# Pacing the pieces of one batch's convolution anew inside an MLP loop

## The chip, the cores and the metric

The kernel runs on one core of a Trainium2 chip. The metric is device time in microseconds (us) of one execution, the median of several. TensorE is called PE here, VectorE DVE, ScalarE ACT, GpSimd POOL and SyncE SP, as in the profile.

## The reference

Two sequences (`B = 2`) of `S = 12480` tokens with 128 channels go through a long convolution with a filter that a small network makes, are gated, and go through an MLP with 2048 hidden units:

```python
h_filt = (np.maximum(pos_emb @ w1, 0) @ w2) * np.exp(-0.01 * pos)[:, None]
u = x * v
y = irfft(rfft(u, 2 * S, axis=1) * rfft(h_filt, 2 * S, axis=0), 2 * S, axis=1)[:, :S]
z = (x * y).reshape(B * S, 128)
h = z @ moe_w_in                       # 128 -> 2048
out = np.maximum(0.01 * h, h) @ moe_w_out
```

## The kernel before

**The convolution** is done as matrix products with constant tables, in two stages and a return. Stage 1 of a batch makes 98-point transforms of 64 columns of tokens, stage 2 joins them across 128 partitions, multiplies them by the filter's spectrum and goes back; the last step of the return, one product per tile (`front`, L679), is part of the MLP's preparation. Batch 0's convolution and the filter's spectrum come first, before any MLP work, together with the preparation of the weights.

**The MLP** runs over `total = 64` tiles of 390 tokens, 32 for each batch (`NT = 32`), and in each tile over `NF = 16` blocks of 128 hidden units. One block is `m1(t, f)` (L689: three matmuls into a tile of tag `mh`, of which there are three; then ACT makes `rh`, the rounded relu, L698, and DVE the remainder `rl`, L699) and `m2` of the block three places earlier (L712 to L714: three matmuls into `acc`). Within a tile other work is inserted by block number `f`, counted from 0: at `f` = 2, 5 and 7 the output of the tile before (`finish`: copy L719; four transposes L723 and the copy L725; the DMAs out L730), at 6 the additions `join(t + 1)` on POOL (L484, L485), at 9 the transposes and copy for `xs` (L671, L673), at 12 the product `yp` (L679), `zf`, `zh` and `zl` (L684 to L686). At the start of a tile `load_tile(t + 1)` puts the loads `g`, `xm` and `cin` (L464 to L473) on SP's queue.

**Batch 1's convolution** is a Python generator, `conv = conv1()`. Each `next(conv)` emits one piece, what stands between two `yield`s. Its first stage works on 16 chunks (`N1`), each in two halves of four pieces; the 16 matmuls of a half (L350) are in its second piece. At a chunk's first piece `fetch_a(c + 1)` puts the next chunk's loads on SP's queue (`ft` L165, `xv` L67 and L69), and `late()` puts the store of the chunk before there (L363). At the fifth piece `mult_a(c + 1)` multiplies the loaded x and v on POOL (L178). The second stage, `conv1b`, works on 25 chunks (`NCH`) of 15 pieces each, between a start of eight pieces and short first and last chunks. In order, with letters that are used below, a chunk's pieces are: O (loads L376 and L379, store L148), A (six matmuls into a pair of PSUM tiles, L416; those of A and F have line L132 in the profile, that of the helper `three`), then per half s of the pair

```python
nc.scalar.mul(us[L, s, :w], up[s][H, :w], -1.0)                      # B (s=0), D (s=1)  L426
nc.vector.tensor_tensor(out=p1[:, s, :w], in0=up[s][:, :w], ...)     # B, D              L427
yield
nc.scalar.copy(us[H, s, :w], up[s][L, :w])                           # C, E              L429
yield
nc.gpsimd.tensor_tensor(out=us[:, s, :w], ...)                       # D, F     L431, L432
```

then F (`back`, six matmuls of the chunk before, into the next pair of PSUM tiles), G and H (two copies, L154), I, J and K (`ph` on ACT L444, `pl` on POOL L445), L, M and N (`split` of the next chunk: `th` on ACT L389 and L393, `tl` on DVE L394; `tl` of the first half in M, of the second in N). A and F use one pair of tiles (tag `cv`, two buffers), so each waits until the other's results have been read.

**The order of work** is written out by hand (`tc.manual_schedule()`): every engine runs its instructions in the order in which the Python code emits them. Eight halves of stage 1, `AHEAD = 32` pieces, are emitted before the MLP's first block. During batch 0's tiles a counter `slots` goes up by one per block, and after each block (behind its `m1`, `m2` and inserted work) as many pieces are emitted as the pace asks for. `pieces` is 498, an estimate of the generator's length; the rest is emitted by the same rule, and by `run(conv)` in tile 31. `SLOTS` is 512.

Of the kernel before, what the change touches and what calls it, by code (L numbers as in the profile page):

```python
# [21 lines left out]
MC1 = 4  # L22
# [5 lines left out]
def tile_conv_mlp(ctx, tc, x, v, pos_emb, w1, w2, w_in, w_out, cf, cr, cg, cb, ci, cw, out):  # L28
# [34 lines left out]
    def load_tokens(t, src, m0, n):  # L63

        full = src[: ROWS * NB, :].rearrange("(a p n) d -> a p n d", p=2, n=HB)
        for r in (slice(0, R0), slice(R0, ROWS)):
            nc.sync.dma_start(out=t[r], in_=full[r, :, m0:m0 + n, :])  # L67
        last = src[ROWS * NB + m0:ROWS * NB + m0 + n, :]
        nc.sync.dma_start(out=t[ROWS:], in_=last[None, None, :, :].to_broadcast([1, 2, n, last.shape[1]]))  # L69
# [34 lines left out]
    def run(g):  # L104
        for _ in g:
            pass
# [51 lines left out]
    with tc.manual_schedule():  # L158
# [3 lines left out]
        def fetch_a(c):  # L162
            ft = s0.tile([128, MC1 * 4 * NA], F32, tag="s0", name="ft1", bufs=3)[:NA].rearrange(
                "a (m p e) -> a m p e", m=MC1, p=2)
            nc.sync.dma_start(out=ft, in_=cf[:, c * MC1:(c + 1) * MC1])  # L165
            xv = []
            for i, src in enumerate((x, v)):
                t = s0.tile([128, 1024], F32, tag=f"s{1 + i}", name="xv1", bufs=3 - i)[:NA, :2 * MC1 * D].rearrange(
                    "a (p m d) -> a p m d", p=2, d=D)
                load_tokens(t, src[1], c * MC1, MC1)  # L170
                xv.append(t)
            got[c] = ft, xv
# [158 lines left out]
        N1 = HB // MC1  # L331
# [121 lines left out]
        pieces = N1 * (MC1 // 2) * 4 + 20 + 14 * NCH  # L453
        A0, A1, A2, A3, A4, A5 = 2, 2, 1, 1, 1, 1
        AHEAD = 4 * (A0 + A1 + A2 + A3 + A4 + A5)
# [5 lines left out]
        def load_tile(t):  # L461
            b, mp = divmod(t, NT)
            g = mlp.tile([NA, 2, 2, 2, NA], F32, tag="g", name="g")
            nc.sync.dma_start(out=g, in_=cg[:, mp])  # L464
            xt = mlp.tile([NA, 2, 2, D], F32, tag="xm", name="xm")
            full = x[b, :ROWS * NB, :].rearrange("(a p n) d -> a p n d", p=2, n=HB)
            for r in (slice(0, R0), slice(R0, ROWS)):
                nc.sync.dma_start(out=xt[r], in_=full[r, :, 2 * mp:2 * mp + 2, :])
            r0 = ROWS * NB + 2 * mp
            nc.sync.dma_start(out=xt[ROWS:, 0], in_=x[b, None, r0:r0 + 2, :])  # L470
            ci_t = mlp.tile([NA, 2, 2, 2, D], F32, tag="cin", name="cin")
            k1 = NA if t else (NCH - 2) * KC
            nc.sync.dma_start(out=ci_t[:k1].rearrange("k r m p d -> k r (m p d)"),  # L473
                              in_=scr2[b][:k1, :, 2 * mp:2 * mp + 2, :].rearrange("k r m e -> k r (m e)"))
            ld[t] = (ci_t, g, xt)

        def join(t):

            ci_t, g, xt = ld[t]
            cp = mlp.tile([NA, 2, 2, 2, D], F32, tag="cp", name="cp", bufs=1)  # L480
            c0, c1 = (ci_t[:, :, :, i, :].rearrange("k r m d -> k (r m) d") for i in range(2))
            o0, o1 = (cp[:, :, :, i, :].rearrange("k r m d -> k (r m) d") for i in range(2))
            eng = nc.gpsimd if t else nc.vector
            eng.tensor_tensor(out=o1, in0=c0, in1=c1, op=ALU.subtract)  # L484
            eng.tensor_tensor(out=o0, in0=c0, in1=c1, op=ALU.add)  # L485
            ld[t] = (cp, g, xt)

        with ExitStack() as st:
# [111 lines left out]
            for c in range(NCH):  # L600
# [14 lines left out]
                for ri in range(2):  # L615
                    for k in range(n):
                        i, j = 64 * (k % 2), ri * n // 2 + k // 2
# [71 lines left out]
        def m1(t, f):  # L689
            zh, zl = z[t]  # L690
            hp = ps.tile([128, TOK], F32, tag="mh", name="mh", bufs=3)
            fs = slice(f * 128, f * 128 + 128)
            nc.tensor.matmul(hp, w_in_h[:, fs], zh, start=True, stop=False)  # L693
            nc.tensor.matmul(hp, w_in_h[:, fs], zl, start=False, stop=False)  # L694
            nc.tensor.matmul(hp, w_in_l[:, fs], zh, start=False, stop=True)  # L695
            rh = sm.tile([128, TOK], F32R, tag="rh", name="rh", bufs=5)
            rl = sm.tile([128, TOK], F32R, tag="rl", name="rl", bufs=5)
            nc.scalar.activation(out=rh, in_=hp, func=AF.Relu)  # L698
            nc.vector.scalar_tensor_tensor(out=rl, in0=hp, scalar=0.0, in1=rh, op0=ALU.max, op1=ALU.subtract)  # L699
            return rh, rl  # L700

        def m2(t, f, r):
            rh, rl = r
            if f == 0:
                zh, zl = z[t]
                ap = ps.tile([128, TOK], F32, tag="acc", name="acc", bufs=2)
                acc[t] = ap
                nc.tensor.matmul(ap, wc_h, zh, start=True, stop=False)
                nc.tensor.matmul(ap, wc_h, zl, start=False, stop=False)
                nc.tensor.matmul(ap, wc_l, zh, start=False, stop=False)  # L710
            ap = acc[t]
            nc.tensor.matmul(ap, w_out_h[:, f, :], rh, start=False, stop=False)  # L712
            nc.tensor.matmul(ap, w_out_h[:, f, :], rl, start=False, stop=False)  # L713
            nc.tensor.matmul(ap, w_out_l[:, f, :], rh, start=False, stop=(f == NF - 1))  # L714

        def finish(t):
            b, mp = divmod(t, NT)
            ot = sm.tile([128, TOK], F32, tag="ot", name="ot")
            nc.scalar.copy(ot, acc.pop(t))  # L719
            yield  # L720
            op = ps.tile([NA, 4, D], F32, tag="io", name="op")
            for p, m, at, n in COLS:
                nc.tensor.transpose(op[:, 2 * p + m, :], ot[:, at:at + NA], ident)  # L723
            os_ = sm.tile([NA, 2, 2, D], F32, tag="os", name="os")
            nc.scalar.copy(os_.rearrange("a p m d -> a (p m) d"), op)  # L725
            yield
            n = b * S
            dst = out[n:n + ROWS * NB, :].rearrange("(a p n) d -> a p n d", p=2, n=HB)
            for r in (slice(0, R0), slice(R0, ROWS)):
                nc.sync.dma_start(out=dst[r, :, 2 * mp:2 * mp + 2, :], in_=os_[r])  # L730
            r0 = n + ROWS * NB + 2 * mp
            nc.sync.dma_start(out=out[None, r0:r0 + 2, :], in_=os_[ROWS:, 0])

        total = B * NT
        SLOTS = NT * NF
        slots, done = 0, AHEAD
# [6 lines left out]
        for _ in range(4 * A5):  # L743
            next(conv)
        fetch_a(4)
        pend = []
        fin = iter(())
        for t in range(total):
            if t + 1 < total and (t + 1) % NT:
                load_tile(t + 1)  # L750
            for f in range(NF):
                pend.append((t, f, m1(t, f)))
                if len(pend) > 3:
                    m2(*pend.pop(0))
                if f == 2 and t:
                    fin = finish(t - 1)
                if f in (2, 5, 7):
                    next(fin, None)
                if t + 1 == NT and f == 6:
                    run(conv)  # L760
                    load_tile(t + 1)
                if t + 1 < total:
                    if f == 6 and (t + 1) % NT:
                        join(t + 1)
                    if f == 9:
                        if (t + 1) % NT == 0:
                            join(t + 1)
                        frt = front(t + 1)
                    if f in (9, 12):
                        next(frt, None)  # L770
                if t < NT:
                    slots += 1
                    while done < AHEAD + (pieces - AHEAD) * slots // (SLOTS - 28):
                        next(conv, None)
                        done += 1
        for q in pend:
# [70 lines left out]
```

## Time and profile before

| | |
|---|---|
| median of 3 runs | 1797.21 us (1795.04 to 1797.37) |
| the profiled execution: its time, its span | 1797.53 us, 1795.5 us |
| PE busy, mean granted clock | 1714.1 us (95% of the span), 0.979 |
| DVE, ACT, POOL busy | 966.5, 892.5, 587.2 us |
| MLP from its first matmul | about 370.9 us to the end |

Lines of the profile name an engine, a line of the code (L693), the operation, its output and inputs, and times in us from the span's start. PE is its matmuls, PEld its weight loads. The end of a matmul is modelled: of matmuls in a row the starts tell the pace. Where a wait is shown, "<-" names what ended it.

### The profile page before, as it was taken

The numbers are of one execution on the slowest core, as the hardware profiler recorded it, in microseconds if no ns is written. First come the engines' busy times: TensorE is split into PE (matmuls) and PEld (weight loads), VectorE is DVE, ScalarE is ACT, GpSimd is POOL, SyncE is SP. The second block draws the span as 40 slices with busy tenths as digits, with TensorE's granted clock in tenths as the row PEclk, the third lists the DMA queues.
The fourth block names the chain that finished last, engine by engine and source line by source line (L and its number), as shares of the span: only waits on it lengthen the run. The fifth ranks groups of instructions, "written<-read, shape, count | busy, mean of one in ns | idle before, by whom it ended". The sixth has DMA issues, their size and how long they took to land.

```text
span 1795.5 us, 29288 instructions
## 1 busy us (share of the span) xinstructions
PE 1714.1 (95%) x10620; PEld 1607.7 (90%) x10620; DVE 966.5 (54%) x1688; ACT 892.5 (50%) x1803; POOL 587.2 (33%) x450
## 2 busy tenths in 40 slices
PE   6787989879999999999999999999999999999998
PEld 6677545479999999999999999999999999999998
DVE  3566788845455555555555544444444444444444
ACT  1222444324445666666666666444444444444444
POOL 3453334213323555555544444211121111211120
PEclk8789999989999999999999999999999999999999
DMA  9898999786756465555555541212211122112210
GB/s 224 244 274 259 310 301 321 235 248 192 216 159 180 121 179 142 140 144 144 144 144 144 141 129 54 77 50 65 60 50 50 54 64 57 51 50 60 65 51 14
DMA packets 147707, 251.77 MB, mean 140 GB/s; under 512 B 10842, under 2 KB 96742, under 8 KB 144492
## 3 DMA queue, kind: packets, MB, share of 16 engines
q1 hardware_dynamic: 127420, 224.21, 44.8%
q10 hardware_dynamic: 20144, 25.69, 4.3%
q8 instruction: 84, 1.38, 0.3%
q14 instruction: 59, 0.48, 0.1%
HBM read 166.37 MB, written 83.43 MB: 139 GB/s over the span
## 4 chain that ended last, share of the span: by engine, by line
PE 84%; DMA 9%; DVE 3%; SPq 2%; issue 1%; ACT 1%; POOL 0%; ACTq 0%; POOLq 0%; DVEq 0%
PE mh L693 10%; PE mh L695 10%; PE mh L694 10%; PE acc L713 10%; PE acc L712 10%; PE acc L714 10%; PE yp L679 6%; PE cv L132 4%; PE cv L350 2%; DMA scr<-o 2%; PE up L117 2%; PE dp L139 2%; DMA xt<-in_x_dram 2%; PE op L723 2%; DMA ft<-in_cf_dram 1%; PE xp L671 1%
## 5 line engine op out<-in xcount | busy, mean ns | idle before, releaser
L699 DVE SCALAR_TENSOR_TENSOR rl<-mh,rh 128x390 fp32r<-128x390 f32 x1024 | 574.9, 564 | 616.6 <-ACT rh L698 614.9
L698 ACT ACTIVATE rh<-mh 128x390 fp32r<-128x390 f32 x1024 | 508.1, 498 | 387.3 <-PE mh L695 369.9
L693 PE MATMUL mh<-zh,w_in_h 128*128 128x390 f32 x1024 | 366.0, 357 | 0.0
L695 PE MATMUL mh<-zh,w_in_l 128*128 128x390 f32 x1024 | 350.2, 342 | 0.0
L694 PE MATMUL mh<-zl,w_in_h 128*128 128x390 f32 x1024 | 349.4, 341 | 0.0
L713 PE MATMUL acc<-rl,w_out_h 128*128 128x390 f32 x1024 | 348.8, 341 | 0.0
L712 PE MATMUL acc<-rh,w_out_h 128*128 128x390 f32 x1024 | 348.3, 340 | 0.0
L714 PE MATMUL acc<-rh,w_out_l 128*128 128x390 f32 x1024 | 348.2, 340 | 0.0
L686 POOL TENSOR_TENSOR zl<-zf,zh 128x390 fp32r<-128x390 f32 x63 | 64.9, 1030 | 706.1 <-ACT zh L685 706.1
L693 PEld LDWEIGHTS mh<-zh,w_in_h 128*128 128x128 f32 x1024 | 194.0, 189 | 2.2 <-DVE rl L699 0.2
L694 PEld LDWEIGHTS mh<-zl,w_in_h 128*128 128x128 f32 x1024 | 193.9, 189 | 2.2 <-DVE zl L686 0.2
L695 PEld LDWEIGHTS mh<-zh,w_in_l 128*128 128x128 f32 x1024 | 194.0, 189 | 0.0
L713 PEld LDWEIGHTS acc<-rl,w_out_h 128*128 128x128 f32 x1024 | 193.9, 189 | 0.0
L714 PEld LDWEIGHTS acc<-rh,w_out_l 128*128 128x128 f32 x1024 | 193.1, 189 | 0.0
L712 PEld LDWEIGHTS acc<-rh,w_out_h 128*128 128x128 f32 x1024 | 193.0, 188 | 0.0
L679 PEld LDWEIGHTS yp<-g,cp 98*128 98x128 f32 x1024 | 123.5, 192 | 0.0
L679 PE MATMUL yp<-g,cp 98*128 98x97 f32 (+1 forms) x1024 | 123.1, 274 | 0.0
L431 POOL TENSOR_TENSOR us<-us,hd 128x512 f32<-128x512 f32 (+1 forms) x50 | 63.6, 1272 | 146.2 <-ACT us L429 146.2
L685 ACT CAST zh<-zf 128x390 fp32r<-128x390 f32 x64 | 33.2, 519 | 148.8 <-DVE zf L684 148.8
L485 POOL TENSOR_TENSOR cp<-cin 98x512 f32<-98x512 f32 x63 | 88.4, 1402 | 0.0
L484 POOL TENSOR_TENSOR cp<-cin 98x512 f32<-98x512 f32 x63 | 81.5, 1293 | 17.5 <-DMA cin<-scr 9.4
L98 ACT COPY a1s<-a 98x384 f32<-98x384 f32 x64 | 30.6, 479 | 110.3 <-PE a L314 67.2
(129 smaller groups left out, 2149.9 us busy)
## 6 DMA issues: line engine op xcount, KB each, us to landing
cin<-scr SPq DMA_DIRECT2D x63, 392.0 KB
hd<-hspec SPq DMA_DIRECT2D x48, 512.0 KB
g<-in_cg_dram SPq DMA_DIRECT2D x64, 300.1 KB
scr<-o SPq DMA_DIRECT2D x32, 588.0 KB
bin<-scr SPq DMA_DIRECT2D x23, 768.0 KB
scr1b<-o SPq DMA_DIRECT2D x32, 392.0 KB
hspec<-hs ACTq DMA_DIRECT2D x48, 256.0 KB
scr<-ct ACTq DMA_DIRECT2D x24, 512.0 KB
```

The lines of the kernel that those rows point to most:

```text
L132: nc.tensor.matmul(dst, u, w, start=(i == 0), stop=(i == 2))
L484: eng.tensor_tensor(out=o1, in0=c0, in1=c1, op=ALU.subtract)
L485: eng.tensor_tensor(out=o0, in0=c0, in1=c1, op=ALU.add)
L679: nc.tensor.matmul(yp[:, at:at + n], ci_t[:, r, m, p, :], g[:, r, p, m, :n], start=(r == 0), stop=(r == 1))
L693: nc.tensor.matmul(hp, w_in_h[:, fs], zh, start=True, stop=False)
L694: nc.tensor.matmul(hp, w_in_h[:, fs], zl, start=False, stop=False)
L695: nc.tensor.matmul(hp, w_in_l[:, fs], zh, start=False, stop=True)
L698: nc.scalar.activation(out=rh, in_=hp, func=AF.Relu)
L699: nc.vector.scalar_tensor_tensor(out=rl, in0=hp, scalar=0.0, in1=rh, op0=ALU.max, op1=ALU.subtract)
L712: nc.tensor.matmul(ap, w_out_h[:, f, :], rh, start=False, stop=False)
L713: nc.tensor.matmul(ap, w_out_h[:, f, :], rl, start=False, stop=False)
L714: nc.tensor.matmul(ap, w_out_l[:, f, :], rh, start=False, stop=(f == NF - 1))
```

## The change

The pace is a function of the block's number `i` (`slots`, 1 to 512). Before, pieces come evenly, 466 over 484 blocks. After, none come up to block 24, the rest of stage 1 (`STAGE1 = 128` less the 32 already emitted) is spread over blocks 24 to 190, and the 370 counted pieces of stage 2 over blocks 190 to 484. What a piece does is not changed.

```diff
         fetch_a(4)
+        STAGE1 = N1 * (MC1 // 2) * 4
+        FROM, TILL = 24, 190
+
+        def pace(i):
+
+            if i < TILL:
+                return AHEAD + (STAGE1 - AHEAD) * max(0, i - FROM) // (TILL - FROM)
+            return STAGE1 + (pieces - STAGE1) * (i - TILL) // (SLOTS - 28 - TILL)
         pend = []
...
                 if t < NT:
                     slots += 1
-                    while done < AHEAD + (pieces - AHEAD) * slots // (SLOTS - 28):
+                    while done < pace(slots):
                         next(conv, None)
                         done += 1
```

## Rows read from the trace of the kernel before

**Rows 1.** The page's first lines: the span, and each engine's busy time with its share and instructions.
```profile
span 1795.5 us, 29288 instructions
PE 1714.1 (95%) x10620; PEld 1607.7 (90%) x10620; DVE 966.5 (54%) x1688; ACT 892.5 (50%) x1803; POOL 587.2 (33%) x450
```

**Rows 2.** Busy time by stretch at the MLP's start: start and end of the stretch, its length, busy us of PE, PEld, DVE, ACT, POOL (with instructions), granted clock of PE, share of the DMA engines, GB/s.
```profile
372.90:377.10 4.20, 0.14 (x1) 0.00 (x0) 1.70 (x4) 0.64 (x2) 2.34 (x1) 1.00 0.95 312
377.10:380.90 3.80, 3.76 (x18) 3.76 (x19) 0.00 (x0) 0.30 (x1) 0.00 (x0) 0.56 0.98 203
384.00:386.00 2.00, 2.00 (x15) 1.99 (x15) 1.50 (x4) 0.99 (x2) 0.00 (x0) 1.00 0.36 78
386.00:388.00 2.00, 2.00 (x18) 2.00 (x17) 0.18 (x1) 0.58 (x2) 0.00 (x0) 1.00 0.91 299
392.00:396.90 4.90, 0.00 (x0) 0.00 (x0) 0.56 (x1) 0.00 (x0) 2.37 (x2) 0.77 0.99 323
396.90:400.80 3.90, 3.88 (x18) 3.88 (x19) 0.00 (x0) 0.07 (x1) 2.41 (x2) 0.50 0.96 221
```

**Rows 3.** The chain of work that ended last, in order of time: start, length, what. From before the MLP's first matmuls to the end of its first tile, and two later tiles' `yp`.
```profile
367.24 7.38 DMA xv<-in_v_dram
374.75 2.35 POOL xv L178
377.14 3.37 PE cv L350 x16
...
394.53 2.34 POOL xv L178
...
396.92 3.73 PE cv L350 x16
...
403.21 1.76 PE yp L679 x16
...
407.14 1.75 PE cv L350 x16
...
1137.96 1.76 PE yp L679 x16
...
1765.17 1.76 PE yp L679 x16
```

**Rows 4.** SP's queue in that stretch (start, length of the issue, transfer), two of the loads of tile 1.
```profile
381.02 2.13 SPq L468 DMA_DIRECT2D xm<-in_x_dram  x2
...
383.66 0.89 SPq L473 DMA_DIRECT2D cin<-scr  x1
```

**Rows 5.** The timeline of the same stretch: the MLP's first matmul, the first `rl` on DVE, the transposes for tile 1 and `join(1)` on POOL.
```profile
370.94 0.43 PE L693 MATMUL mh<-zh,w_in_h 128*128 128x390 f32 x1
...
373.11 0.55 DVE L699 SCALAR_TENSOR_TENSOR rl<-mh,rh 128x390 fp32r<-128x390 f32 x1
...
390.36 0.50 PE L671 MATMUL xp<-ident,xm 97*128 97x97 f32 x4
...
396.82 1.26 POOL L484 TENSOR_TENSOR cp<-cin 98x512 f32<-98x512 f32 x1
...
398.04 1.26 POOL L485 TENSOR_TENSOR cp<-cin 98x512 f32<-98x512 f32 x1
```

**Rows 6.** The waits between 400 and 1130 us, by who waits for whom: us in total, times, the longest.
```profile
PEld cv L132 <- ACT us L429: 4.2, 11, 0.8
PEld cv L132 <- DVE tl L394: 0.8, 1, 0.8
...
ACT us L429 <- DVE p L427: 7.8, 30, 0.3
```

**Rows 7.** The timeline of ACT, DVE and PE around pieces B to F of one chunk of stage 2 (start, length; in brackets the idle time before and what ended it).
```profile
855.38 0.60 ACT L426 ACTIVATE us<-cv 64x512 f32<-64x512 f32 x1
855.64 0.34 PE L693 MATMUL mh<-zh,w_in_h 128*128 128x390 f32 x1
856.00 0.50 ACT L698 ACTIVATE rh<-mh 128x390 fp32r<-128x390 f32 x1
856.07 0.69 DVE L427 TENSOR_TENSOR p<-cv,hd 128x512 f32<-128x512 f32 x1 [1.18 <-ACT us L426]
...
856.71 0.34 PE L693 MATMUL mh<-zh,w_in_h 128*128 128x390 f32 x1
856.79 0.58 ACT L429 COPY us<-cv 64x512 f32<-64x512 f32 x1 [0.29 <-DVE p L427]
...
859.15 0.48 PE L132 MATMUL cv<-ph,mi_h 128*128 128x512 f32 x1
...
859.27 0.58 ACT L429 COPY us<-cv 64x512 f32<-64x512 f32 x1 [0.23 <-DVE p L427]
...
859.93 0.48 PE L132 MATMUL cv<-ph,mi_h 128*128 128x512 f32 x1
```

**Rows 8.** The timeline around the start of stage 2: the last store of stage 1, the first load that reads it back, and the first `th`.
```profile
551.60 0.83 SPq L363 DMA_DIRECT2D scr1b<-o  x2
...
556.07 0.36 SPq L376 DMA_DIRECT2D bin<-scr1b  x1
...
559.78 0.62 ACT L389 CAST th<-bin 128x512 fp32r<-128x512 f32 x1 [1.25 <-DMA bin<-scr1b]
```

**Rows 9.** Groups of instructions by line over the whole span: busy us, mean ns of one.
```profile
L699 DVE SCALAR_TENSOR_TENSOR rl<-mh,rh 128x390 fp32r<-128x390 f32 x1024 | 574.9, 564 | 616.6 <-ACT rh L698 614.9
L394 DVE TENSOR_TENSOR tl<-bin,th 128x512 fp32r<-128x512 f32 x48 | 50.9, 1061 | 0.0
```

## The prediction

> **What bounds the kernel now.** I read the page's totals first: PE is busy 95% of the span [rows 1], so only PE's idle time and its slow clock are there to be won, and the pieces that move are the same work wherever they stand. The chain of waits and the stretches then show where PE loses time. In the MLP's first tile it stands still twice, 4.1 us before 377.14 and 4.9 us before 396.92, each time in front of the matmuls of a half of stage 1 that wait for a product on POOL, which waits for a load [rows 3]. During both waits the DMA engines are 95% to 99% busy, and after both the granted clock is at half, 1.2 of 2.4 GHz, for some 4 us [rows 2]: 16 matmuls that take 1.75 us later take 3.37 and 3.73 us here [rows 3]. From 400 us to the end of batch 0's part the waits of PE that the profile names are small, 4.2 us in front of PE's weight loads in 11 of stage 2's pieces F, and one of 0.8 us in a piece A [rows 6]. In batch 1's part a tile without pieces takes (1765.17 - 1137.96) / 31 = 20.23 us [rows 3], and nothing changes there.
>
> **The start, where time is won.** By the old pace the first matmuls of a moved half come after block 3, then after 7 and 11; by the new one the first come after block 28. So three halves, 3 x 1.75 = 5.25 us, leave the first tile and are paid later. From the MLP's first matmul, 370.94 [rows 5], to the end of tile 1's `yp`, 403.21 + 1.76 = 404.97 [rows 3], there are 34.0 us. The work in it: a block takes 1.07 us, by two neighbouring starts of L693 [rows 7]; 13 `m1` and 10 `m2` are 12.3 us, the three extra matmuls with `wc` 0.5, the transposes about 0.4, `yp` 1.76, together 15.0. With the halves that makes 20.25, so 13.8 us are lost now.
>
> They don't all go away, because tile 1's own loads become late next. SP's order up to them is not changed, so they are issued when they are now: `xm` from 381.02 to 383.15, `cin` from 383.66 [rows 4]. PE comes to the transposes of `xm` earlier: `m1` of block 3 needs an `mh` tile that DVE frees at 373.66 [rows 5]; from there one `m1`, `wc`, one `m2` and six blocks are 8.0 us, so 381.7. The DMA engines fall to 36% between 384 and 386 and then move 299 GB/s [rows 2]; I read this as the end of `xm` and the start of `cin`, and take 385.5 for `xm` landed and 388.2 for `cin` (estimates). PE waits 3.8 us, nearly as long as in the first wait of now, so I charge the same half clock: 3.8 us at 0.56 [rows 2] lose about 1.7. Then 385.5 + 0.4 + 3 blocks + 1.7 = 390.8 at `yp`. `join(1)` is no longer behind a product that waits for a load, starts at 388.2 and needs twice 1.26 us [rows 5]: 390.8 as well. `yp` ends at 392.6. Won: 404.97 - 392.6 - 5.25 = **7.1 us**. Bounds: with `cin` as slow as the load of v, 7.4 us from its issue [rows 3], it is 4.3; with no wait at tile 1 at all, 13.0.
>
> Behind this, tile 2's loads go out at once, as nothing stands before them, and chunk 5's loads go out near block 23, behind the output of tile 0, for matmuls in block 42: some 25 us against the 7.4 that a load took under full DMA load [rows 3]. I cost the rest of stage 1 at nothing; it has 166 blocks where it had 98.
>
> **Stage 2, where time is lost.** It gets 294 blocks where it had 384. 370 counted pieces in 294 blocks are 1.26 per block, where 0.96 came: about every fourth block now gets two, which never happened. The work is the same, but chains over ACT, DVE and PE lose blocks in which PE did something else.
>
> *Pieces B to F.* ACT scales, DVE multiplies, ACT copies, for each half, and F writes into the tiles that they read. In [rows 7] this chain takes from 855.38 to 859.85, 4.47 us, with a relu of 0.50 between every two operations, while PE does four blocks, 4.28 us, and comes to F's second half 0.78 us after its first (0.69 without a wait). PE waited a little there. A chain that starts on time (ACT 0.7 us behind the last matmul of B's `m1`) reaches the end of E's copy 5.2 us after that matmul, and PE reaches F's second half after 0.5 + 4.3 + 0.7 = 5.5: a slack of 0.3. With two of the pieces in one block PE comes 1.07 earlier. What ACT saves depends on the pair. Writing out the new formula for the 24 chunks with an F gives: A with B 5 times, B with C 5, C with D 5, D with E 5, E with F 4 times. C with D: one relu less in the chain, 0.5, so PE waits about 0.25. B with C or D with E: one relu less, but the copy stands right behind its own half's scaling and waits for all of DVE's product, 0.69 [rows 7], with nothing to fill it, so about nothing is saved: 0.75. E with F: nothing saved, 0.75. A with B: F is as far as before, 0. Sum: 14 x 0.75 + 5 x 0.25 = 11.7 us. Where other ACT work of a tile falls in between (`zh`, which waits for `yp`) it is up to twice that, where PE has inserted work (f = 3, 5, 9) it is nothing; I let these cancel. Of the 4.2 us of now [rows 6] all is in the 11.7: **+7.5 us**. Bounds: 0, if weights and matmuls hide it as the modelled ends suggest for most of now's waits, to +13.
>
> That the copy waits for DVE's product is in the trace, 30 times, 7.8 us [rows 6], although both only read the same tile. The Trainium skill (PSUM — Partial Sum Buffer, section "PSUM bank collisions raise a hardware error") says that two engines may not access one PSUM bank in the same partitions at once, two reads included, and that a dependency has to keep them apart. By this rule the wait stays however closely the pieces stand, and the time is the forecast's; were it an accident of the old spacing, B with C and D with E would cost nothing and the time would be 1794.0. The trace agrees as far as it shows the wait; no run here shows a collision.
>
> *Piece A* needs N's `tl`. Before, A was two or three blocks behind N; now in 11 of 25 chunks one block. M and N put two `tl` of 1.06 us between DVE's `rl` of 0.56 [rows 9], 1.62 per block against PE's 1.07; one block away I work out 0.45 us of wait, spared in about half of the cases by inserted PE work: 11 x 0.2 = **+2.2 us** (0, as nearly always now, to 5).
>
> *The change of stages.* The first `th` waits for stage 1's last store to land and be read back: from 551.60 to 559.78, 8.2 us, ACT waits 1.25 [rows 8] and PE does not. `th` came six blocks behind stage 1's last piece, with 0.7 us of inserted PE work; it now comes five blocks behind with none, 1.75 us earlier. ACT, with the relus queued behind `th`, waits 3.0. Three `mh` tiles let PE go on for about 1.3 us: **+1.7 us** (0 to 3).
>
> **Sum.** 1797.53 (the profiled execution) - 7.1 + 7.5 + 2.2 + 1.7 = 1801.8. The median of the runs shown is 0.3 lower: 1801.5.
>
> **Rivals.**
> 1. *The crowding is hidden.* PE's small waits of now hardly show (the chain of waits has none of them as a piece of its own), and ACT with 50% and DVE with 54% have room on the mean. Then the gain at the start is all there is, less up to 1.7 at the change of stages: 1790.4 to 1792. Against it: in [rows 7] ACT is never idle but for the two waits, so the room is elsewhere. It decides if PE's waits at L132 stay under 6 us in all. 18%.
> 2. *Both are about equal.* The crowding costs half, 5.7 us: 1797.2 - 7.1 + 5.7 = 1795.8. For it: half of the doubled pieces meet inserted PE work. 25%.
> 3. *Less is won at the start*, the lower bound of 4.3, and the crowding is whole: 1804.3. For it: a load took 7.4 us under full DMA load, and tile 1's loads stand behind the same queue. 15%.
> 4. The forecast, 1799 to 1804: 42%, of which I put 12 points below 1800.8.
>
> A difference under 0.2%, 3.6 us, can hardly be told from none here. Faster than 1793.6 is rival 1, 18%. Within 0.2% are rival 2 and the forecast's lower end, 37%. Slower than 1800.8 are rival 3 and the rest of the forecast, 45%. The range from 1791 to 1806 leaves out some 10% on each side: the early bound of 13.0 with little crowding, and all the upper bounds together (-4.3 + 13 + 5 + 3, 1813.9).
>
> **What would show it.** At the start: no matmuls of L350 before block 28; PE idle before tile 1's transposes, some 4 us, half clock behind it, and `yp` ending near 392.6. In stage 2: PE's waits for ACT L429 some 12 us in more than 15 of the chunks, and for DVE L394 in about ten, a few tenths each; tiles of 20.23 + 3.73 (20.1 pieces, 12 of each 15 being matmuls' worth 0.23 us) + 0.5 us. At the change of stages: ACT L389 waiting 3 us for the load. Wrong would make it: `xm` and `cin` landing elsewhere than estimated; ACT running far enough ahead in the doubled blocks; a wait that I have not seen, as POOL behind a product that waits for its load.

## The result, and the profile after

The changed kernel takes 1819.31 us (median of four, 1817.66 to 1823.43) where the kernel before took 1797.29 beside it: 1.0129 times as long, 95% interval 1.0114 to 1.0145. The forecast was 1801.5 and its range ended at 1806; even all its upper bounds together, 1813.9, lie below the result. A second series gave 1.0164 (1.0142 to 1.0185).

The page of the kernel after begins with the lines that answer to [rows 1]. PE is busy 9.4 us longer over the same 10620 matmuls; the rest of 21.1 us is idle time of PE.

```profile
span 1816.6 us, 29283 instructions
PE 1723.5 (95%) x10620; PEld 1609.8 (89%) x10620; DVE 970.7 (53%) x1688; ACT 894.2 (49%) x1803; POOL 588.0 (32%) x450
```

To place the 21 us I take the distance from one tile's `yp` to the next in the trace of PE and subtract the work in it: 20.235 us for a tile without pieces (by [rows 3], 20.23), 1.75 for each half of stage 1 in it, 0.23 for each matmul L132 (0.117 for a narrow one of the last chunk). What remains is lost. At `yp(31)` the kernel after is 1138.27 - 1117.53 = 20.74 us behind:

- start, to `yp(1)`: 386.79 after, 403.05 before, with 5.25 us of work moved behind it: 11.0 us **won** (forecast 7.1);
- the rest of stage 1: 0.5 lost (forecast 0);
- the two tiles around the change of stages: 12.6 lost, nothing before: **12.7** (forecast 1.7);
- the other tiles of stage 2: 20.9 lost, 2.4 before: **18.5** (forecast 9.7).

From there to the end both take the same. These four numbers come from one trace of each kernel.

**The start after.** The chain that ended last, as in [rows 3]. The two stops in front of L350 are gone; half clock still comes once, over `yp(0)` and the half behind it (3.37 and 3.41 us in place of 1.76 and 1.75).

```profile
365.82 3.37 PE yp L679 x16
369.19 3.41 PE cv L350 x16
...
383.39 0.34 PE xp L671 x4
...
386.68 1.24 POOL cp L485
387.96 1.13 PE yp L679 x8
```

And SP's queue, as in [rows 4]: `xm` is issued 3.3 us earlier than in the trace of before. Nothing that the change moves stands ahead of it on that queue, and the load of `g` just ahead, at 375.36 where before has 377.43, is already 2.1 us earlier. One execution differs from another by that much; the other runs below show how far it goes.

```profile
377.75 2.22 SPq L468 DMA_DIRECT2D xm<-in_x_dram  x2
```

**Stage 2 after.** The waits between 400 and 1150 us, by who waits for whom (us in total, times, the longest), answer to [rows 6].

```profile
POOL cp L484 <- DMA cin<-scr: 33.2, 6, 19.2
...
PEld cv L132 <- ACT us L429: 17.1, 16, 1.8
PEld cv L132 <- DVE tl L394: 13.9, 17, 1.4
ACT us L429 <- DVE p L427: 13.7, 33, 0.8
...
PE cv L132 <- ACT us L429: 10.5, 14, 1.4
...
PE cv L132 <- DVE tl L394: 7.8, 12, 1.1
ACT th L389 <- DMA bin<-scr1b: 5.7, 1, 5.7
```

Before, PE's weight loads waited 11 times in front of F, 0.8 us at most, and nearly all of it under matmuls still running (PE itself stood twice there, 0.6 us in all); now PE itself stands 14 times, up to 1.4 us. The wait for `tl`, one before, comes 17 times. In distances between the starts of PE's matmuls from `yp(14)` to `yp(31)`, F's first matmuls account for 11.9 us over their work (1.4 in all of before's stage 2) and those with `tl` for 6.6 (0.8).

**The change of stages after.** SP's queue, to be held against [rows 8].

```profile
656.59 1.88 SPq L363 DMA_DIRECT2D scr1b<-o  x2
662.19 0.35 SPq L376 DMA_DIRECT2D bin<-scr1b  x1
...
663.86 0.51 SPq L464 DMA_DIRECT2D g<-in_cg_dram  x1
...
666.25 0.85 SPq L473 DMA_DIRECT2D cin<-scr  x1
```

The read-back L376 waits on SP for the store, and the loads of tile 13 (`g` to `cin`) stand behind it. The timeline of the same place:

```profile
666.39 0.62 ACT L389 CAST th<-bin 128x512 fp32r<-128x512 f32 x1 [5.68 <-DMA bin<-scr1b]
...
667.06 0.51 PE L132 MATMUL cv<-th,mb_h 128*128 128x512 f32 x1 [2.73 <-ACT th L389]
...
675.33 1.30 POOL L484 TENSOR_TENSOR cp<-cin 98x512 f32<-98x512 f32 x1 [19.25 <-DMA cin<-scr]
```

ACT, with the relus behind `th`, stands 5.7 us; PE stands 2.7; POOL's join waits for `cin`, issued at 666.25, until 675.33, and POOL starts the first chunk's products behind it. By stretches (columns as in [rows 2]) PE is busy 16.2 of 20 us, at a mean granted clock of 0.83, and then 16.6 of 20; the line by itself is the part of it in which the clock was at half:

```profile
640.00:660.00 20.00, 20.00 (x129) 19.89 (x128) 10.69 (x19) 9.67 (x20) 1.03 (x1) 1.00 0.15 42
660.00:680.00 20.00, 16.18 (x76) 15.00 (x75) 6.83 (x12) 8.28 (x17) 4.59 (x4) 0.83 0.91 214
680.00:700.00 20.00, 16.59 (x92) 14.64 (x91) 9.08 (x16) 11.90 (x24) 11.63 (x10) 1.00 0.52 134
```

```profile
670.00:675.00 5.00, 5.00 (x16) 4.72 (x16) 1.76 (x4) 1.95 (x4) 0.00 (x0) 0.52 1.07 239
```

In distances between matmul starts, the 12.6 us of these two tiles are 2.9 in front of the first matmul with `th`, 1.4 in front of the first with `tl`, some 2.9 at half clock behind them, up to 675, and 5.5 from 684 on, at `rl`, `tl` and F of the first chunks.

### The profile page after: what moved, and what is told of

It reads as the page before. It is cut to its first block, busy times and chain, and to the rows that moved or that the text cites. A ratio compares the mean times of both kernels' runs of the same rounds, so it can differ in the third digit from the quotient of the medians.

```text
span 1816.6 us, 29283 instructions
## 1 busy us (share of the span) xinstructions
PE 1723.5 (95%) x10620; PEld 1609.8 (89%) x10620; DVE 970.7 (53%) x1688; ACT 894.2 (49%) x1803; POOL 588.0 (32%) x450
## 4 chain that ended last, share of the span: by engine, by line
PE 80%; DMA 6%; DVE 6%; ACT 3%; issue 2%; SPq 1%; POOL 1%; DVEq 0%; POOLq 0%; ACTq 0%
PE mh L693 9%; PE mh L695 9%; PE mh L694 9%; PE acc L713 9%; PE acc L712 9%; PE acc L714 9%; PE yp L679 6%; PE cv L132 3%; DMA xt<-in_x_dram 3%; PE cv L350 3%; PE up L117 2%; PE dp L139 2%; PE op L723 2%; PE a L314 1%; DMA ft<-in_cf_dram 1%
## 5 line engine op out<-in xcount | busy, mean ns | idle before, releaser
L484 POOL TENSOR_TENSOR cp<-cin 98x512 f32<-98x512 f32 x63 | 83.5, 1325 | 43.7 <-DMA cin<-scr 33.2
L485 POOL TENSOR_TENSOR cp<-cin 98x512 f32<-98x512 f32 x63 | 86.1, 1367 | 0.0
## 6 DMA issues: line engine op xcount, KB each, us to landing
cin<-scr SPq DMA_DIRECT2D x63, 392.0 KB
scr1b<-o SPq DMA_DIRECT2D x32, 392.0 KB
```

## The experiments

Fourteen more runs were made, of thirteen further kernels and of the changed kernel once more (after_again). The table gives the ratio to the kernel before with its interval, and the places above: the start of `yp(1)` (with 5.25 added where the new pace has moved three halves behind it), and what was lost in stage 1, around the change of stages and in the rest of stage 2, from one profiled execution each.

| kernel | ratio (95%) | `yp(1)` | stage 1 | change | stage 2 |
|---|---|---|---|---|---|
| before | 1 | 403.1 | 0.0 | -0.1 | 2.4 |
| after | 1.0129 (1.0114-1.0145) | 392.0 | 0.4 | 12.6 | 20.9 |
| after_again | 1.0164 (1.0142-1.0185) | 396.8 | 0.1 | 12.8 | 22.5 |
| start_alone | 0.9970 (0.9959-0.9981) | 396.0 | -0.2 | -0.1 | 2.8 |
| crowd_alone | 1.0123 (1.0106-1.0140) | 401.9 | -0.1 | 4.0 | 20.1 |
| change_held | 1.0122 (1.0107-1.0137) | 394.7 | 0.1 | 8.8 | 18.2 |
| till_148 | 1.0025 (1.0010-1.0040) | 391.0 | 0.0 | 0.0 | 11.1 |
| till_180 | 1.0078 (1.0052-1.0104) | 393.0 | -0.1 | 3.7 | 18.0 |
| till_196 | 1.0127 (1.0112-1.0143) | 392.8 | 0.1 | 9.2 | 22.6 |
| split_early | 1.0071 (1.0056-1.0086) | 392.7 | 0.1 | 7.9 | 13.3 |
| reordered | 1.0026 (1.0011-1.0040) | 391.0 | 0.5 | 7.8 | 5.4 |
| pl_on_dve | 1.0114 (1.0097-1.0132) | 396.4 | 0.5 | 11.0 | 15.5 |
| one_fetch | 0.9960 (0.9948-0.9973) | 395.5 | 0.0 | -0.1 | 2.3 |
| reord_100 | 0.9946 (0.9934-0.9958) | 389.0 | -0.2 | -0.1 | 0.2 |
| even_pace | 0.9959 (0.9945-0.9974) | 395.7 | 0.0 | 0.9 | 2.6 |
| best | 0.9922 (0.9909-0.9936) | 384.6 | -0.2 | -0.1 | -0.2 |

**The two halves of the change, each alone.** The first keeps the empty first 24 blocks, but ends stage 1 at block 100 as before:

```diff
-        FROM, TILL = 24, 190
+        FROM, TILL = 24, 100
```

> The pause in the first 24 blocks alone: stage 1 is spread over blocks 24 to 100, and stage 2 comes at its old pace (0.964 pieces per block from block 100). Theory: the start wins 10.6 us, the change of stages and the crowded second stage of the changed kernel cost 31.2 us, and the two have nothing to do with each other: 1797.3 - 10.6 = 1786.7, plus at most 3 for a first stage that now gets 1.26 pieces per block. Rival: the gain at the start is lost again when the loads of stage 1 come closer together (1.26 pieces per block ask some 230 GB/s), then PE stands before L350 again: 1793 to 1798.

The second has the old pace in stage 1, ends it at block 100 and holds stage 2 back to block 190:

```diff
             if i < TILL:
-                return AHEAD + (STAGE1 - AHEAD) * max(0, i - FROM) // (TILL - FROM)
+                return min(STAGE1, AHEAD + (pieces - AHEAD) * i // (SLOTS - 28))
```

> The crowded second stage alone: the old pace to block 100, where stage 1 is done, no pieces to block 190, then stage 2 at the changed kernel's pace. Theory: start as before, change of stages and stage 2 as in the changed kernel: 1797.3 + 31.2 = 1828, with PE's weight loads waiting some 17 us for ACT L429 and 14 us for DVE L394. Rival: the loss comes from the slower first stage or from what the pause does to the queues, not from stage 2's pace: 1797 to 1803.

They measured 1787.9 and 1816.9 us beside 1793.4. The empty first blocks are a gain by themselves, with stage 1 at 1.26 pieces a block behind them and nothing lost there; but by the times it is 5.5 us (3.4 to 7.4 by the interval), half of the 10.6 that the first trace had led to expect. In its trace the start went almost as forecast: `xm` issued at 381.22 (forecast 381.02), a wait of PE for it (3.8), half clock behind it (a granted clock of 0.56 from 385.6 to 389.5), `yp` from 390.71 (390.8).

```profile
381.22 1.95 SPq L468 DMA_DIRECT2D xm<-in_x_dram  x2
```

```profile
385.56 0.58 PE L671 MATMUL xp<-ident,xm 97*128 97x97 f32 x4 [3.43 <-DMA xm<-in_x_dram]
390.71 1.93 PE L679 MATMUL yp<-g,cp 98*128 98x97 f32 x16
```

The second kernel lost 23.5 us where 31.2 were expected. Away from the change of stages stage 2 lost as much as in the changed kernel, 20.1 and 20.9; the two tiles at the change lost 4.0 in place of 12.6, with the same pieces in the same blocks from 190 on. SP's queue has the same order there, with the loads of tile 13 behind store and read-back:

```profile
656.01 0.83 SPq L363 DMA_DIRECT2D scr1b<-o  x2
660.51 0.35 SPq L376 DMA_DIRECT2D bin<-scr1b  x1
...
662.18 0.51 SPq L464 DMA_DIRECT2D g<-in_cg_dram  x1
```

But the data of the store were ready at 550.5, so it went out in block 184, as soon as SP came to it, and `th` began at 669.94, 13.9 us behind it, without a wait. In the changed kernel DVE ends the last of these data at 656.56, the store goes out in block 192, and ACT comes to `th` 4.1 us later. By stretches, as above, nothing is lost up to 680:

```profile
660.00:680.00 20.00, 20.00 (x122) 19.65 (x121) 10.91 (x20) 11.66 (x24) 5.33 (x5) 1.00 0.92 229
680.00:700.00 20.00, 17.70 (x99) 16.12 (x98) 9.16 (x17) 11.96 (x25) 12.01 (x10) 1.00 0.45 111
```

So stage 2's pace by itself costs the 20 us and 4.0 at the change; the other 8.6 there come with a store that is late for `th`, and with stage 1's last pieces just ahead of it, in which the two kernels differ as well.

**The rate.** Only the block of the change is moved, which sets stage 2's rate: 1.10, 1.22, 1.26 and 1.28 pieces a block for 148, 180, 190 and 196.

```diff
-        FROM, TILL = 24, 190
+        FROM, TILL = 24, 148      # till_180: 180; till_196: 196; after_again: 190
```

> The changed kernel once more, on the chip of the three runs beside it: 1.3% over the kernel before (1.0129 was measured). What it is to tell besides is the start. It won 11.0 us there against the first profile of before (the projections of tile 1 start at 386.79 where they started at 403.05, with 5.25 us less work of the convolution ahead of them), while stage one spread to block 100 from the same block 24 won 7.1. If the difference comes from the loads ahead of tile 1, which are the same in both kernels, it varies from run to run and these projections start anywhere from 386 to 392. If it belongs to the longer spread of stage one, they start at 386 to 388 again. The change of stages should cost 12 to 13 us over tiles 12 and 13 again, and stage two some 19 us.

> The change of stages at block 148: stage two at 370/336 = 1.101 pieces a block, with 9 doubled pairs among B to F (19 in the changed kernel) and A one block behind N in 3 chunks (10). Theory, by the rate: the 18.6 us that stage two lost come with what is over one piece a block, so 18.6 x 0.101/0.259 = 7.3 us are left, the change of stages costs 1 to 3 us as in the kernel before, and the start stays won: 10 + 11 = 21 us under the changed kernel, 1794 to 1797 on a chip where before takes 1793, the same as before. Rival, a threshold: with the chains of ScalarE and VectorE full above one piece a block, each chunk loses the same 0.7 us or so as soon as its pieces are crowded at all; then 15 us and more are left and it takes 1802 to 1805.

> Only the change of stages is moved, from block 190 to block 180. Stage two then runs at 370/304 = 1.217 pieces a block (1.259 in the changed kernel), with 18 doubled pairs among pieces B to F (19). The store and the read-back would be issued ten blocks earlier, from block 4 of tile 11 on, and not just ahead of the loads of tile 13. Theory: the 12.6 us at the change of stages are the tile's loads queued behind the store and the read-back on SP, so that the time is 9 to 12 us less there, and 15 to 18 us are left in stage two: some 12 to 14 us under the changed kernel, 1802 to 1804 on a chip where before takes 1793. Rival: the read-back's wait costs the same wherever it falls, since every engine has filled its slack by then; then only stage two's rate gives 1 to 3 us, and it takes 1813 to 1815.

The start of the same code moved by 4.7 us between the two traces of the changed kernel, so it varies from run to run. They measured 1823.3, 1797.2 and 1807.1 us beside 1792.6. Stage 2 loses 2.8 (at 0.96), 11.1, 18.0 and 20.9 to 22.5 us: over the 2.8 that is 8.3 / 0.101 = 82, 15.2 / 0.217 = 70 and 18.1 to 19.7 / 0.259 = 70 to 76 us for each piece a block over one. The threshold that the rival had, 15 us and more at 1.10, is out. The price is roughly proportional to that excess, each point being one trace; till_196, at 1.28, fits with 19.8 / 0.285 = 69, and change_held below, at 1.29 behind its pause, is cheaper, 15.4 / 0.290 = 53. Till_180 took 1807.1, between its theory and its rival.

**The change of stages.** In the next kernel only stage 2's first piece, with the last store and the first loads, is emitted in the eight blocks from 190 on; then stage 2 goes on a little faster.

```diff
-            return STAGE1 + (pieces - STAGE1) * (i - TILL) // (SLOTS - 28 - TILL)
+            if i < TILL + 8:
+                return STAGE1 + (i > TILL)
+            return STAGE1 + 1 + (pieces - STAGE1 - 1) * (i - TILL - 8) // (SLOTS - 36 - TILL)
```

> The changed kernel, but at block 190 only the first piece of stage 2 is emitted (the last store and the first loads), and the next seven blocks get none; stage 2 then has 286 blocks instead of 294. Theory: the two tiles at the change lose 12.6 us because the first th stands on ACT before its load has landed (5.7 us) and everything behind it is late: th comes 7 blocks, 7.5 us later, so about 11 us of it go, and the denser stage 2 costs 0.5 to 1 more: 1808 to 1809. Rival: these tiles lose time because their pieces are crowded, whatever the load does: 1817 to 1820.

Measured 1815.4, a miss. The wait of `th` was gone, yet 8.8 us were lost, 3.8 of them with PE standing for `xm`. In this kernel's rows of SP and PE the loads of tile 13 still stand behind store and read-back:

```profile
664.07 0.35 SPq L376 DMA_DIRECT2D bin<-scr1b  x1
...
666.30 1.32 SPq L468 DMA_DIRECT2D xm<-in_x_dram  x2
...
674.65 0.53 PE L671 MATMUL xp<-ident,xm 97*128 97x97 f32 x4 [3.79 <-DMA xm<-in_x_dram]
```

So the store was put behind these loads (block 196):

> The changed kernel with the change of stages six blocks later, at block 196, so that the last store of stage one and its read-back are issued behind the loads of tile 13 and not ahead of them. The rate of stage two grows a little, from 1.259 to 370/288 = 1.285. Theory: the 12.6 and 12.8 us lost over the two tiles at the change are for the most part these loads queued behind store and read-back; 3 to 5 us are left there (4.0 where the store was long done, 3.7 with the change at block 180), stage two loses 1 to 2 us more, and it is 6 to 8 us under the changed kernel. Rival: a late change costs by itself, since its chains have to start up at this rate, whatever stands on SP's queue: then 10 us and more are lost there, and the time is the changed kernel's or up to 2 us longer.

Measured 1817.0 beside 1794.1, a miss for the theory that the queue is most of it. The loads of tile 13 now went out at 644.5, ahead of the store; neither `xm` nor `th` held PE for more than 1 us, the granted clock stayed at 1.00, and 9.2 us were lost all the same: in the distances between matmuls 4.0 in front of `tl`, 2.1 in front of `mh` for a late `rl`, 1.4 in F, 1.2 in front of `th`. The store is late for `th` here too, and ACT stands:

```profile
ACT th L389 <- DMA bin<-scr1b: 3.5, 1, 3.5
```

So the place of the tile's loads on the queue is not most of it. What it is worth can't be read from 12.6 - 9.2 = 3.4 us, since the rate and the place of the first chunks in a tile differ too. The experiment that keeps both, the second of the two halves above, puts 8.6 us on the late store, with the wait of `th` and the half clock behind it, and 4.0 on the first chunks' own waits. Why 9.2 us are lost here and 3.7 with the change at block 180, where `th` waited 2.9 us, is open.

**The order of the pieces.** Two kernels keep the changed kernel's pace. In the first the next chunk's split is issued before J and K:

```diff
+                if c + 1 < NCH:
+                    yield from split(c + 1)
                 if c < NCH:
                     for s in range(2):
                         nc.scalar.copy(ph[:, s, :w], p1[:, s, :w])
...
-                if c + 1 < NCH:
-                    yield from split(c + 1)
             late()
```

> The changed kernel with the pieces of split (th and tl of the next chunk, L to N) emitted before those of ph and pl (J, K), so that N lies three pieces further ahead of A. Theory: PE's wait for tl (13.9 us before its weight loads, 10.9 us between matmul starts) is a matter of how many blocks lie between N and A: it falls under 2 us, the wait for ACT L429 stays at 17, and the time is 1808 to 1811. Rival: ACT has too much work in these blocks whatever the order; then the wait moves from DVE L394 to ACT L429 or to the relus, and the time is 1816 to 1820.

In the second the same two lines stand further ahead, in front of `if c:` and the back transform, so that L, M and N come between E and F:

> The pace of the changed kernel, 1.259 pieces a block, with the order of a chunk's pieces changed: the next chunk's split (L, M, N) is issued ahead of the back transform (F to I) and no longer behind J and K, so three pieces lie between the last reader of the shared PSUM pair (E) and the matmuls that want it (F), and eight between the split and the matmuls that read it (A). Theory: the 18.6 us of stage two are the two waits, F for the copies of ScalarE (17.1 us in the trace of the changed kernel) and A for tl (13.9), and neither has a cause of its own in the rate; both go to under 3 us, stage two loses at most 5, and the time is 13 to 17 us under the changed kernel: 1800 to 1804 where before takes 1793, with the 12.6 us at the change of stages still there. Rival: at 1.26 pieces a block ScalarE and VectorE are full, and the waits turn up at the MLP's own blocks (its first matmuls waiting for rl and th) or at the join; then 8 to 12 us are left and the time is within 8 us of the changed kernel's.

Measured 1806.4 beside 1793.4, a little under its theory's range, and 1798.0 beside 1792.6, under it too. The waits of the first, in which `tl` no longer holds A while F waits as before:

```profile
PEld cv L132 <- ACT us L429: 18.8, 17, 1.9
...
PEld cv L132 <- DVE tl L394: 1.9, 2, 1.4
```

and of the second, where the wait for L429 has left the list:

```profile
PEld mh L693 <- DVE rl L699: 9.7, 18, 1.3
...
PEld cv L132 <- DVE tl L394: 1.9, 2, 1.4
```

The same pieces at the same pace, in another order, lose 5.4 us in stage 2 in place of 20.9. What is left is for the most part the MLP's own blocks waiting for `rl` (PE itself stood 4.0 us for it in all of stage 2): there the rate itself may show.

**What makes `tl` late.** One tile's view in the trace of the kernel after, from 660 to 760 us (count; ns: least, median, most): half and more of the `tl` take 0.68 us, the longest 1.78, where the mean over the kernel before is 1.06 [rows 9]. In the whole trace of after, the 19 `tl` beside which POOL does nothing take 0.68 us at most, and the 31 that meet one of POOL's `pl` or join operations (L445, L484, L485) 0.83 to 2.58.

```profile
L394 DVE TENSOR_TENSOR tl<-bin,th x11: 681/682/1781, 667.9 to 759.1; 128x512 fp32r<-128x512 f32 x11
```

A long one, in the timelines of POOL, ACT, DVE and PE:

```profile
704.12 1.29 POOL L485 TENSOR_TENSOR cp<-cin 98x512 f32<-98x512 f32 x1
705.37 1.75 POOL L445 TENSOR_TENSOR pl<-p,ph 128x512 fp32r<-128x512 f32 x1
```

```profile
703.62 0.64 ACT L393 CAST th<-bin 128x512 fp32r<-128x512 f32 x1
...
704.26 1.70 DVE L394 TENSOR_TENSOR tl<-bin,th 128x512 fp32r<-128x512 f32 x1
...
706.36 1.31 DVE L394 TENSOR_TENSOR tl<-bin,th 128x512 fp32r<-128x512 f32 x1
...
707.72 0.50 PE L132 MATMUL cv<-tl,mb_h 128*128 128x512 f32 x1 [0.67 <-DVE tl L394]
```

The first `tl` ends 0.55 us after POOL's L485, POOL's `pl` then ends 1.16 after `tl`, and the second `tl` 0.55 after `pl`: each looks as if it did its work only when the other was done. The Trainium skill (SBUF — State Buffer, section "SBUF: two separate sides") says that DVE, in an operation with two SBUF inputs, and GpSimd share a pair of ports that one of them holds for a whole instruction. The rows agree: each of the 31 ends 0.55 us behind the end of one of these operations (0.28 the only half tile among them). To see whether this is what delays A, `pl` was taken off POOL:

```diff
-                        nc.gpsimd.tensor_tensor(out=pl[:, s, :w], in0=p1[:, s, :w], in1=ph[:, s, :w],
+                        nc.vector.tensor_tensor(out=pl[:, s, :w], in0=p1[:, s, :w], in1=ph[:, s, :w],
```

> The changed kernel with the subtraction that makes pl (L445) on VectorE and no longer on POOL; the rest is as it was. In the trace of the changed kernel tl (L394, DVE) takes 0.68 us where POOL stands idle and 1.3 us and more where POOL works on pl or the join at the same time; of the 6.6 us that PE loses in front of matmuls with tl in stage two, 5.4 follow a tl of over 1 us. Theory: the late tl is the meeting of these two engines. Without pl on POOL most tl take 0.68 us; in stage two PE loses under 2.5 us in front of tl, the waits named DVE tl L394 fall from 13.9 us to under 7 (the first chunk's stay), and stage two loses 16 to 18 us in place of 20.9 and 22.5. Rival: tl is late because ScalarE makes th late and DVE has rl ahead of it; then two more operations of 0.68 us for DVE in pieces J and K make it worse, the waits stay at 12 us or more, and stage two loses as much or more.

Measured 1815.7 beside 1794.1. No `tl` meets one of POOL's operations any more. In its rows `tl` has a mean of 0.669 us and its wait is down from 13.9 to 3.8 us, although DVE has more to do; stage 2 lost 15.5 us, a little less than expected.

```profile
L394 DVE TENSOR_TENSOR tl<-bin,th 128x512 fp32r<-128x512 f32 (+1 forms) x50 | 33.0, 669 | 0.0
```

```profile
PEld cv L132 <- ACT us L429: 16.4, 15, 1.8
...
PEld cv L132 <- DVE tl L394: 3.8, 7, 1.4
```

**A faster kernel.** First the kernel before without line 745, which fetches chunk 4 a second time:

```diff
-        fetch_a(4)
```

> The kernel before with line 745 left out, its pace untouched. Chunk 4's tokens and matrices are already fetched by the convolution's own loop (lines 337 and 338) when line 745 fetches them a second time, just ahead of the loads of tile 1; nothing of the computation is left out. The 8.4 us that the kernel before loses at the start are two waits of a half's first matmul for POOL's product L178 of tokens just landed (4.4 and 4.9 us in a trace with before's start). Theory: the first is the second fetch's, so that 3 to 5 us are won, 1788.5 to 1790.5 where before takes 1793, and the second, for chunk 5, stays. Rival: POOL's product of chunk 4 is late because POOL is late, and both waits stay: 1792 to 1794. Second rival: all that follows on the queue comes 4 us earlier too, the second wait goes with the first, and it takes 1784 to 1786, as much as all that the new pace won at the start.

Measured 1785.3 beside 1793.2: as much as in the second rival, but by its second half alone. In PE's timeline the first wait of [rows 3] stays, 4.43 us, and it is the second, 4.96, that is gone, with all loads behind line 745 issued some 8 us earlier.

```profile
376.91 3.53 PE L350 MATMUL cv<-xv,ft 98*98 98x128 f32 x16 [4.43 <-POOL xv L178]
385.21 1.91 PE L350 MATMUL cv<-xv,ft 98*98 98x128 f32 x16
```

Then the new start with the new order, stage 1 ending at block 100 (reord_100); the same without line 745 (best); and that with the change at block 114 (even_pace):

```diff
-        FROM, TILL = 24, 190
+        FROM, TILL = 24, 100      # even_pace: 24, 114
```

> The changed kernel with stage one ending at block 100 as in the kernel before, and with the order of pieces of the run with the split ahead of the back transform. The start alone gave 0.997 of the time before, with 2.1 us still lost in stage two, all of it in its first six tiles. Theory: the order takes these to under 1 us, 0.9955 to 0.9965. Rival: at 0.96 pieces a block the order no longer matters, 0.997.

> As the run beside it (stage one from block 24 to block 100, split ahead of the back transform), and without the second fetch of chunk 4. Theory: with no piece in the first 24 blocks nobody waits for chunk 4 at the start (the tiles 0 to 1 lose -0.8 to 2.2 us in the runs with that start), so that it gives at most 2 us more: 0.9945 to 0.9965, at or just under the run beside it. Rival: the second fetch also holds tile 1's loads back, and the 0 to 2.2 us vary with it: then 0.993 to 0.9945.

> As the last, with the change of stages at block 114, so that stage one runs at 1.07 and stage two at exactly 1.00 pieces a block. By the counts no two pieces fall into one block in stage two, as at 0.96, and it should be the same as the last within 2 us; a rate at which every block has a piece, with no empty one, costs 2 to 5 us more if the chains need the empty blocks to catch up.

Measured 1784.7, 1779.2 and 1786.9 beside 1793.2. The order takes stage 2's loss at 0.96 pieces a block from 2.8 to 0.2 us. The version called best is 0.8% under the kernel before. It gained more than its theory and its rival had. Its gain over reord_100 shows in the profile at the start alone (two kernels, the stretch from 360 to 375 us of best and then of reord_100):

```profile
360.00:375.00 15.00, 13.73 (x90) 13.21 (x91) 9.55 (x18) 6.17 (x12) 2.76 (x2) 1.00 0.91 259
```

```profile
360.00:375.00 15.00, 14.34 (x70) 13.92 (x69) 7.97 (x15) 4.22 (x9) 2.39 (x1) 0.66 0.94 267
```

PE did 90 matmuls there at a granted clock of 1.00 against 70 at 0.66. Whether leaving out the fetch causes that was not repeated, and even_pace, which also leaves it out, fell to half clock from 370 to 375 us; the two intervals just touch. Even_pace is 7.7 us slower than best. In the traces, one of each, its stages lose 3.9 us more, so a block without a piece now and then may be worth something even where no two pieces share one; the rest stands at its start, which varies.

## Why the prediction was wrong

The direction of both effects was right, and the rows named the right places: the start wins, F and A lose, the change of stages loses. The sizes of the losses were not: 7.5 + 2.2 + 1.7 = 11.4 us were forecast and 18.5 + 12.7 = 31.2 came. More than half of what is missing is the change of stages.

- **The change of stages**, +1.7 forecast, 12.7 measured, far over the bound of 3: the term that failed most. Its first step is that `th` comes 1.75 us earlier and ACT waits 3.0. Counted from the store, ACT was ready for `th` after 8.2 - 1.25 = 6.9 us before and after 9.8 - 5.7 = 4.1 now, 2.8 us earlier, and store and read-back took 9.8 us in place of 8.2: a wait of 5.7. The second step is that three `mh` tiles leave 1.7 of this on PE. PE lost 2.9 there and 1.4 more in front of `tl`, then some 2.9 at half clock, which the sum charged for a wait at the start and left out here. The rest, 5.5 us behind 684, is what the first chunks lose by their pace, which the sum has under F and A. Where the store was early only such waits were left, 4.0 us.
- **Piece A**, +2.2 forecast, +5.8 measured outside the change (6.6 less 0.8), over the bound of 5. That A comes one block behind N in 11 of 25 chunks was right, and these are the chunks that wait for the most part. The failed step is the 1.06 us for a `tl`, the mean in [rows 9]: it lies between 0.68 us alone and up to 2.58 beside POOL, and the long ones hold PE for 0.3 to 2 us where 0.2 was charged on the mean. Taking `pl` off POOL removed nearly all of it, and so did three more pieces between N and A.
- **Pieces B to F**, +7.5 forecast, +10.5 measured (11.9 less 1.4, at F's first matmuls alone), within the bound of 13. Here the mechanism holds pair by pair. Over all of stage 2 PE lost in front of F, by the distances between matmul starts, nothing for A with B (0 forecast), 3.3 us for B with C (3.75), 1.1 for C with D (1.25), 3.6 for D with E (3.75) and 4.8 for E with F (3.0): 12.8 in all, where 11.7 were worked out. What was mis-sized besides E with F is what was taken off: the 4.2 us of now are waits of PE's weight loads, of which only 1.4 showed on PE. Three other pieces between E and F take the wait away. That the copy waits for DVE's product holds: 33 times, 13.7 us, where it was 30 times and 7.8 [rows 6]. The rule of the Trainium skill that the prediction cites (PSUM — Partial Sum Buffer, section "PSUM bank collisions raise a hardware error") would keep that wait however close the pieces are, and the trace agrees; no run here shows a collision.
- **The start**, 7.1 forecast, 11.0 in the first trace, 7.0 in the trace of the start alone and 5.5 by its times. The two stops went as told. "They are issued when they are now" can't be told from one execution: over the eleven with this start and with line 745, `xm` was issued between 374.5 and 382.4, PE waited 1.9 to 3.4 us for it in five of them and not at all in six, among these the first trace, where half clock ahead of block 3 held the MLP back. `yp(1)` stood between 389.0 and 396.8, 6.3 to 14.1 us won against the one trace of before. So the 11.0 is for a part luck, and the start alone, with `xm` where it was forecast, went as forecast. The upper bound of 13.0 comes to some 12.6 by the prediction's own numbers (381.7 + 0.4 + 3.2 + 1.76 = 387.1 at the end of `yp`).
- **The rivals.** "The crowding is hidden" is out: the waits at L132 that should have stayed under 6 us came to some 21 on PE. "Both about equal" is close to what the change at block 148 does (1.0025), not block 190. "Less is won at the start" has the times of the start alone between its 4.3 and the 7.1 forecast, but would have come to 1804.3, far from what was measured. The rivals that were missing are a `tl` that meets POOL, and a change of stages that stops ACT long enough to stop PE. F and A, though, do not hang on each other: without A's wait F's stayed as it was (18.8 and 16.4 us of weight loads' waits in place of 17.1).

## What to carry to other kernels

Interleaved work is free only as long as each engine's chain has room in the few blocks where it stands: here, with ACT at 50% and DVE at 54% on the mean, each piece a block over one cost some 70 to 80 us, and an order with other pieces between the last reader of a buffer and its next writer gave back most of it at the same pace. A moved step whose data are stored and read back has to be given the time of that way, 8 to 10 us here, before the first reader stands in front of other work; and a mean duration is to be looked at for two values before it is put into a chain. And a start full of waits for loads may hold a load that nobody needs: one deleted line gave 0.4%.

## What the runs showed of the hardware

`tl` on DVE, two SBUF inputs, takes 0.68 us alone (19 times in the trace of after) and 0.83 to 2.58 beside POOL's `pl` and join (31 times); POOL's `pl` took 1.75 in place of 1.30 in the same meeting. The same code at the start placed `yp(1)` at 386.79 and at 391.50 in two executions, and the granted clock over its first blocks was at half in some traces and full in others, though the program ahead of it was the same.
